# Four edits to a fused attention and MLP kernel: weight groups 3, 4, 3, 3, 3, relays on GpSimd, loads on SyncE, one early load on two queues

## The chip, the cores and the metric

The kernel runs on one core of a Trainium2 chip. The metric is the device time of one execution in microseconds; the median of three runs stands for the kernel. The trace is that of one profiled execution of the kernel before.

The engines are named as in the profile: PE is TensorE's matmul side and PEld its weight load, DVE is VectorE, ACT is ScalarE, POOL is GpSimd, SP is SyncE. SP, ACT and POOL also start DMA transfers, each from a queue that is worked through in order: an issue that has to wait holds up all that stand behind it on its engine.

## The reference

Talking-heads attention and, on its output, a two-matrix MLP with a parametrised ReLU. B = 4 batches, H = 12 heads, S = 448 positions, D = 64; the MLP has 1792 tokens, a model width of 768 and an inner width of 2048.

```python
scores = scale * np.matmul(q, k.transpose(0, 1, 3, 2))
scores = np.einsum('bhij,hg->bgij', scores, w_pre)        # mix over heads
scores = scores - np.max(scores, axis=-1, keepdims=True)
attn = np.exp(scores)
attn = attn / (np.sum(attn, axis=-1, keepdims=True) + 1e-09)
attn = np.einsum('bhij,hg->bgij', attn, w_post)           # mix over heads
x = np.matmul(attn, v)                                    # [B, H, S, D] -> [B*S, H*D]
h = x @ w_in
g = np.maximum(h, 0.0) + alpha * np.minimum(h, 0.0)
out = g @ w_out
```

The MLP's weights and alpha are given as float64.

## The kernel before, in words

**Attention.** A batch is cut into four chunks of query positions (120, 120, 120 and 90), 16 chunks in all. For a chunk, six score matmul pairs (Q, `qk`, L317) fill a tile `st` by way of PSUM copies (S, `qk_out`, L330). To mix over heads, the heads must lie on partitions: a relay (L, `relay`, L337) is an SBUF to SBUF DMA that brings ten positions of 12 heads, 120 rows of 448 floats (210 KB), from `st` into one of eight buffers `sr`. Two relays feed one mix (M, L344). There are 180 relays and 90 mixes. Behind a mix come the row maximum on DVE (R, L349), the exponential on ACT (E, L356), the normalised second mixing matrix on DVE (N, L362 to L366), the second mix with transposition on PE (P, `post`, L378), and copies into the tile `at` (A, L390). With all groups of a chunk done, V (`pv`, L400) multiplies by v; its result is split into a high and a low part (L414, L416) and stored in DRAM (`store_x`, L421).

The order of all of this is written out ahead by `plan`, a list scheduler with costs in us and priorities. It treats DMA as one engine; `emit` then issues each operation on a real queue. A relay goes to SP or POOL in turn (`relay_q`, L660). Loads of k (`load_k`, L279), q (`load_q`, L292) and v (`load_v`, L302) and the first three weights (`fetch`, L444) go to POOL; stores of x and of converted weights, and the loads of x and of converted weights for the MLP (L518, L548), go to SP. The planner gives a load a time, but on the chip a load waits only for its buffer and for what stands ahead of it in its queue. k has four buffers, q three, v three halves, the raw weights two.

Ahead of the plan the first chunk's q and all k of batch 0 are loaded by halves on SP and ACT (`hw`, L459 to L463). The second chunk's q follows on SP alone (L488).

**MLP.** The inner width is 16 blocks f of 128. A unit u is one f for one batch bl: `l1` (L577, 18 matmuls) computes h, four operations on ACT and DVE (L590 to L596) make g, `l2` (L615, 18 matmuls) adds to six PSUM accumulators. The f are grouped (`FGROUPS`, L39): a group runs all its f for one batch, adds the accumulators into SBUF (`l2_out`, L627), and goes to the next batch. There are 64 units in either grouping. On PE the order is l1(u), l2(u - 1), l1(u + 1) and so on. Unit u first needs f as the groups list it.

A weight is rounded from float64 to float32 and split into a high and a low part on DVE and ACT. The first NPRE = 3 blocks are made during the attention. The other 13 are made during the MLP by `convert2`: for each of w_in and w_out seven DVE operations (L59 to L65) and one split (L539 on ACT, L541 on DVE), so 16 steps to a block. There is room for five blocks. Block f with f % 5 = 0 takes the place of f - 5; the blocks with f % 5 = 1 and 2, and those with 3 and 4, share a tile and take the places of f - 5 and f - 4 together (`w_free`, L532). A tile is taken between the rounding and the split of w_in, when the last unit of the old blocks has been issued.

The steps are put between the units by credit. What a unit needs and is not yet done is issued ahead of it:

```python
def conv_ops(us):
    credit = min(credit + us, 4.0)
    while credit > 0 and conv_at < NFC:
        r = next(conv2)              # None: the tile is not free yet
        ...
        credit -= 0.95
...
    while conv_at <= units[u][2] and units[u][2] >= NPRE:
        conv_ops(0.95)               # ahead of l1(u)
...
            conv_ops(0.95)           # within the unit
        conv_ops(2.6)                # behind it
```

Raw weights of `convert2` are fetched by POOL (`fetch_w`, L427), two passes ahead. The x of a batch is loaded from DRAM into one of three tiles (`load_x`, L511) when the first unit of a batch before it starts.

Of the kernel before, what the change touches and what calls it, by code (L numbers as in the profile page):

```python
# [20 lines left out]
DM, DFF = 768, 2048  # L21
# [14 lines left out]
RAHEAD = 3  # L36
LAG = 2
WARM = (12, 8)
FGROUPS = [[0, 1, 2], [3, 4, 5], [6, 7, 8], [9, 10, 11], [12, 13, 14, 15]]  # L39
NPRE = 3  # L40
NWP = 4
NXS = 3
# [179 lines left out]
def talking_heads_prelu(ctx: ExitStack, tc: tile.TileContext, q, k, v, w_pre, w_post, mask, w_in, w_out, alpha, out):  # L222
    nc = tc.nc
# [48 lines left out]
    def load_k(b, kk, hfs=(-1, 0, 1), parts=((0, 2),), dmas=None):  # L272
        if -1 in hfs:
            k_t[b, kk] = kp.tile([128, 2, S], F32, tag="k", name=f"k{b}_{kk}")
        t = k_t[b, kk]
        for p0, p1_ in parts:
            for hf in [i for i in hfs if i >= 0]:
                dma = dmas[hf] if dmas else nc.gpsimd
                dma.dma_start(out=t[64 * hf:64 * hf + 64, p0:p1_, :],  # L279
                              in_=k[b, :, (NP * hf + 2 * kk + p0) * S:(NP * hf + 2 * kk + p1_) * S])  # L280

    def load_q(ci, hfs=(-1, 0, 1), dmas=None):
        b, c = chunk_list[ci]
        c0, cn = CHUNKS[c]
        if -1 in hfs:
            q_t[ci] = qp.tile([128, NP * CW], F32, tag="q", name=f"q{ci}")
            pad = 64 + MIN_M - cn
            if pad > 0:
                nc.gpsimd.memset(q_t[ci][:, NP * cn:NP * cn + pad], 0.0)
        for hf in [i for i in hfs if i >= 0]:  # L290
            dma = dmas[hf] if dmas else nc.gpsimd
            dma.dma_start(out=q_t[ci][64 * hf:64 * hf + 64, :NP * cn],  # L292
                          in_=q[b, :, QOFF[c] + NP * hf * cn:QOFF[c] + NP * (hf + 1) * cn])

    def load_v(b, hx, s):
        if s < 0:
            v_t[b, hx] = vp.tile([128, NS, DM // 2], F32, tag="v", name=f"v{b}_{hx}")
            return
        n = min(S - 128 * s, 128)
        if n < 128:  # L300
            nc.gpsimd.memset(v_t[b, hx][n:, s, :], 0.0)
        nc.gpsimd.dma_start(out=v_t[b, hx][:n, s, :], in_=v[b, 128 * s:128 * s + n, hx * DM // 2:(hx + 1) * DM // 2])  # L302

    u_t = {}

# [28 lines left out]
    def relay(n, dma, sr):  # L334
        ci, r = groups[n]
        sr_t[n] = sr_b[sr]
        dma.dma_start(out=sr_t[n][SR0:SR0 + GP], in_=s_t[ci][r:CHUNKS[chunk_list[ci][1]][1]:CHUNKS[chunk_list[ci][1]][1] // GI])  # L337
# [98 lines left out]
    conv = {}  # L436

    def fetch(i, k):
        f, x = half(i)
        if k < 0:  # L440
            conv[i] = [cvp.tile([128, DM], I64, tag="cr", name=f"cr{f}_{x}")]
            return
        n = slice(k * DM // NWP, (k + 1) * DM // NWP)
        nc.gpsimd.dma_start(out=conv[i][0][:, n], in_=(w_in, w_out)[x][f][:, n])  # L444

    def conv_op(i, j):
        if j == 0:
# [9 lines left out]
    with tc.manual_schedule():  # L457
# [3 lines left out]
        load_k(0, 0, parts=((0, 1), (1, 2)), dmas=hw)  # L461
        load_k(0, 1, dmas=hw)
        load_k(0, 2, dmas=hw)  # L463

        warm = start.tile([128, S], F32R, tag="warm", bufs=1, name="warm")
        nc.vector.memset(warm.bitcast(F32), 0.0)
# [16 lines left out]
        for i, w in enumerate((w_pre, w_post)):  # L483
            for p in ((SR0, 64), (0, 64))[i]:
                nc.gpsimd.dma_start(out=mask_sb[p:p + HP, i], in_=mask[:HP, :HI, :])
                nc.gpsimd.dma_start(out=wb[p:p + HP, i, :],
                                    in_=w.rearrange("(o h) g -> o h g", o=1).to_broadcast([HI, H, H]))
        load_q(1, dmas=(nc.sync, nc.sync))  # L488
        nc.gpsimd.dma_start(out=alpha_sb, in_=alpha)
        P2 = {}  # L490
        p2 = ctx.enter_context(ExitStack())
# [153 lines left out]
        turns = [0]  # L645
# [11 lines left out]
            )  # L657

        def relay_q(n, sr):
            relay(n, (nc.sync, nc.gpsimd)[turns[0] % 2], sr)  # L660
            turns[0] += 1
            if turns[0] == 1:
                matrices()
            if turns[0] == 2 * RAHEAD:
                nc.vector.tensor_scalar(out=oma, in0=alpha_sb, scalar1=-1.0, scalar2=1.0, op0=ALU.mult, op1=ALU.add)
# [118 lines left out]
```

## Time and profile before

| what | us |
|---|---|
| median of 3 runs | 864.59 (863.59 to 872.91) |
| profiled execution | 864.0 |
| its span | 861.5 |
| PE busy | 810.8 |
| DVE busy | 576.6 |
| ACT busy | 341.8 |
| POOL busy | 134.5 |

The span is the time between the first and the last instruction in the trace; 2.5 us of the execution lie around it. A window row gives for a stretch of the span the busy time of each engine with its number of instructions, the clock that TensorE was granted (1.00 is 2.4 GHz, 0.50 is 1.2 GHz), the mean busy share of the 16 DMA engines and what they moved. A wait row names the engine and line that waited, what released it, and the total, the number and the longest. A timeline row gives start, duration, instruction and, in brackets, the idle time before it with its releaser. The chain follows the last instruction back to what released it, step by step.

### The profile page before, as it was taken

Reading aid. Unit: us, or ns where it says so; the run is one execution under the profiler, and the core shown is the slowest. Engines: PE = TensorE matmul, PEld = TensorE weight load, DVE = VectorE, ACT = ScalarE, POOL = GpSimd, SP = SyncE. Lnnn points to the kernel's source line nnn. Section 1 sums busy time; section 2 is a strip of 40 time slices with the busy share of each in tenths; the row PEclk is TensorE's granted clock in tenths of the full one; section 3 lists DMA queues with packets and bytes.
Section 4 is the critical chain, followed back from the end, with each engine's and each line's share of the span. In section 5 each row is a group of like instructions: output and inputs, shape, how many; then the busy total and the mean of one; then the engine's idle time right before and its main releaser. Section 6 shows DMA issues by size and latency. Waiting matters only on the chain.

```text
span 861.5 us, 23937 instructions
## 1 busy us (share of the span) xinstructions
PE 810.8 (94%) x10380; PEld 654.2 (76%) x10380; DVE 576.6 (67%) x1029; ACT 341.8 (40%) x712; POOL 134.5 (16%) x243
## 2 busy tenths in 40 slices
PE   7679999989899999899999999999999999799998
PEld 3336666666566667689999999999999998689997
DVE  4678888877678878766555666676667646961332
ACT  3456767757666775542222211212121212111111
POOL 3443334323333221000000000000000000000000
PEclk9799999999999999999999999999999999989999
DMA  6899778969786778978211511251125111240111
GB/s 144 205 206 255 217 221 219 243 195 246 206 218 191 215 212 248 261 202 294 74 37 37 202 38 37 74 202 37 38 74 170 69 37 37 74 159 33 65 65 64
DMA packets 75036, 125.36 MB, mean 146 GB/s; under 512 B 33876, under 2 KB 63588, under 8 KB 74932
## 3 DMA queue, kind: packets, MB, share of 16 engines
q1 hardware_dynamic: 57636, 63.91, 24.5%
q0 software_dynamic: 16896, 59.07, 24.1%
q8 instruction: 81, 1.33, 0.7%
q10 hardware_dynamic: 400, 0.87, 0.4%
q14 instruction: 23, 0.19, 0.1%
HBM read 66.16 MB, written 18.92 MB: 99 GB/s over the span
## 4 chain that ended last, share of the span: by engine, by line
PE 77%; DVE 8%; DMA 7%; ACT 5%; issue 2%; SPq 0%; POOL 0%; DVEq 0%; ACTq 0%
PE h L577 27%; PE acc L615 26%; PE x L400 8%; PE pa L378 7%; DMA sr<-st 5%; PE m L344 5%; PE s L317 4%; DVE at L390 2%; ACT at L390 2%; ACT e L356 2%; DVE nm L349 2%; ACT st L330 1%; DMA k<-in_k_dram 1%; DVE ao L627 1%; DMA q<-in_q_dram 0%
## 5 line engine op out<-in xcount | busy, mean ns | idle before, releaser
L577 PE MATMUL h<-x,w 128*128 128x448 f32 x1152 | 250.5, 370 | 6.5 <-ACT w L539 6.4
L615 PE MATMUL acc<-g,w 128*128 128x448 f32 x1152 | 245.5, 366 | 0.6 <-DVE g L596 0.6
L577 PEld LDWEIGHTS h<-x,w 128*128 128x128 f32 x1152 | 217.3, 189 | 28.8 <-ACT w L539 6.8
L615 PEld LDWEIGHTS acc<-g,w 128*128 128x128 f32 x1152 | 216.1, 188 | 20.0 <-DVE g L596 1.0
L378 PEld LDWEIGHTS pa<-r,e 64*64 64x64 f32 x5040 | 98.5, 135 | 68.4 <-DVE at L390 27.5
L592 DVE SCALAR_TENSOR_TENSOR t<-t,oma,h 128x448 f32<-128x448 f32 x64 | 43.5, 680 | 153.8 <-ACT t L590 153.8
L590 ACT ACTIVATE t<-h 128x448 f32<-128x448 f32 x64 | 34.9, 545 | 263.6 <-PE h L577 263.6
L356 ACT ACTIVATE e<-m,nm 128x448 f32<-128x448 f32 x180 | 112.7, 634 | 40.2 <-DVE nm L349 26.5
L378 PE MATMUL pa<-r,e 64*64 64x60 f32 x5040 | 105.4, 223 | 18.3 <-issue 6.7
L349 DVE TENSOR_REDUCE nm<-m 128x2 f32<-128x896 f32 x90 | 97.1, 1083 | 12.0 <-PE m L344 11.8
L344 PE MATMUL m<-sr,wk 64*64 64x448 f32 x720 | 92.1, 563 | 11.6 <-DMA sr<-st 10.0
L317 PE MATMUL s<-k,q 64*64 64x448 f32 (+2 forms) x768 | 97.5, 564 | 5.5 <-ACT e L356 2.4
L400 PEld LDWEIGHTS x<-at,v 128*64 128x64 f32 x1536 | 74.5, 137 | 20.1 <-ACT e L356 11.2
L337 POOL DMA_DIRECT2D sr<-st x90 | 55.5, 618 | 201.6 <-PE m L344 135.5
L400 PE MATMUL x<-at,v 128*64 128x120 f32 (+1 forms) x1536 | 81.4, 263 | 2.9 <-ACT e L356 2.9
L390 DVE COPY at<-pa 128x480 f32<-128x480 f32 x89 | 57.7, 655 | 34.8 <-ACT at L390 31.3
L330 ACT COPY st<-s 120x896 f32<-120x896 f32 (+1 forms) x68 | 61.5, 908 | 26.7 <-PE s L317 25.6
L390 ACT COPY at<-pa 128x480 f32<-128x480 f32 x91 | 51.2, 570 | 51.3 <-PE pa L378 38.5
L594 ACT CAST g<-t 128x448 fp32r<-128x448 f32 x64 | 36.3, 567 | 53.3 <-DVE t L592 53.3
L627 DVE TENSOR_TENSOR ao<-ao,acc 128x448 f32<-128x448 f32 x96 | 52.7, 615 | 1.7 <-PE acc L615 1.7
L317 PEld LDWEIGHTS s<-k,q 64*64 64x64 f32 (+2 forms) x768 | 29.4, 130 | 30.4 <-issue 12.2
L344 PEld LDWEIGHTS m<-sr,wk 64*64 64x64 f32 (+1 forms) x720 | 24.8, 135 | 33.4 <-ACT e L356 9.3
(51 smaller groups left out, 539.7 us busy)
## 6 DMA issues: line engine op xcount, KB each, us to landing
sr<-st SPq DMA_DIRECT2D x90, 210.0 KB
sr<-st POOLq DMA_DIRECT2D x90, 210.0 KB, 5.5
x<-x SPq DMA_DIRECT2D x12, 1344.0 KB
cr<-in_w_in_dram POOLq DMA_DIRECT2D x13, 768.0 KB, 4.5
cr<-in_w_out_dram POOLq DMA_DIRECT2D x13, 768.0 KB, 4.6
x<-xe SPq DMA_DIRECT2D x48, 180.0 KB
x<-x SPq DMA_DIRECT2D x24, 224.0 KB
out_dram<-ao SPq DMA_DIRECT2D x24, 224.0 KB
```

Of the source, the lines that this page charges most:

```text
L317: nc.tensor.matmul(ps[i0:i1, hf, :S], q_t[ci][r, p * cn + i0:p * cn + i1], k_t[b, p // 2][r, p % 2, :], start=True, stop=True)
L330: copy(dst[:cn, p], u_t.pop(("qk", ci, p))[:cn, :, :S])
L337: dma.dma_start(out=sr_t[n][SR0:SR0 + GP], in_=s_t[ci][r:CHUNKS[chunk_list[ci][1]][1]:CHUNKS[chunk_list[ci][1]][1] // GI])
L344: nc.tensor.matmul(ps[hf:hf + 64, u, :S], wk[r, :], g[r, :], start=True, stop=True)
L349: nc.vector.tensor_reduce(out=nm, in_=m_t[m][:, :, :S], axis=AX.X, op=ALU.max, negate=True)
L356: nc.scalar.activation(out=e_t[m][:, u], in_=m_t[m][:, u, :S], func=AF.Exp, bias=nm_t[m][:, u:u + 1], scale=1.0, accum_out=se_t[m][:, u:u ...
L378: nc.tensor.matmul(dst[:, :, HI * u:HI * u + HI], e[h, u, 64 * jb:64 * jb + 64], r[h, u].rearrange("p (h i) -> p h i", h=H), start=True, s ...
L390: copy_on[eng](dst, pa[:, g, :NS * GP].rearrange("p (s i) -> p s i", i=GI))
L400: nc.tensor.matmul(ps[64 * t:64 * t + 64, 0, cl * CW:cl * CW + cn], v_t[b, hx][:, s, (2 * cl + t) * D:(2 * cl + t + 1) * D], a_t[ci][:, s, ...
L577: nc.tensor.matmul(ps[:, :S], w[:, tw, cc * 128:(cc + 1) * 128], x[:, tx, cc, :], start=(i == 0), stop=(i == 3 * NCC - 1))
L615: nc.tensor.matmul(accs[c][:, :S], w[:, tw, c * 128:(c + 1) * 128], g[:, tg], start=(f == fs[0] and i == 0), stop=(f == fs[-1] and i == 2))
L627: nc.vector.tensor_tensor(acc_sb[c, bl], acc_sb[c, bl], accs[c][:, :S], ALU.add)
```

## The change

- The groups of f become 3, 4, 3, 3, 3 blocks instead of 3, 3, 3, 3, 4.
- All relays are issued by POOL; before, SP and POOL took turns.
- All loads of k, q and v in the plan and the loads of the first three weights are issued by SP; before, by POOL. `fetch_w`, for the other 13 weights, stays on POOL.
- The second chunk's q is issued right behind the k loads, one half on SP and one on ACT; before, both halves on SP.

```diff
--- before.py
+++ after.py
@@ -36,7 +36,7 @@
 RAHEAD = 3
 LAG = 2
 WARM = (12, 8)
-FGROUPS = [[0, 1, 2], [3, 4, 5], [6, 7, 8], [9, 10, 11], [12, 13, 14, 15]]
+FGROUPS = [[0, 1, 2], [3, 4, 5, 6], [7, 8, 9], [10, 11, 12], [13, 14, 15]]
 NPRE = 3
 NWP = 4
 NXS = 3
@@ -275,7 +275,7 @@
         t = k_t[b, kk]
         for p0, p1_ in parts:
             for hf in [i for i in hfs if i >= 0]:
-                dma = dmas[hf] if dmas else nc.gpsimd
+                dma = dmas[hf] if dmas else nc.sync
                 dma.dma_start(out=t[64 * hf:64 * hf + 64, p0:p1_, :],
                               in_=k[b, :, (NP * hf + 2 * kk + p0) * S:(NP * hf + 2 * kk + p1_) * S])
 
@@ -288,7 +288,7 @@
             if pad > 0:
                 nc.gpsimd.memset(q_t[ci][:, NP * cn:NP * cn + pad], 0.0)
         for hf in [i for i in hfs if i >= 0]:
-            dma = dmas[hf] if dmas else nc.gpsimd
+            dma = dmas[hf] if dmas else nc.sync
             dma.dma_start(out=q_t[ci][64 * hf:64 * hf + 64, :NP * cn],
                           in_=q[b, :, QOFF[c] + NP * hf * cn:QOFF[c] + NP * (hf + 1) * cn])
 
@@ -299,7 +299,7 @@
         n = min(S - 128 * s, 128)
         if n < 128:
             nc.gpsimd.memset(v_t[b, hx][n:, s, :], 0.0)
-        nc.gpsimd.dma_start(out=v_t[b, hx][:n, s, :], in_=v[b, 128 * s:128 * s + n, hx * DM // 2:(hx + 1) * DM // 2])
+        nc.sync.dma_start(out=v_t[b, hx][:n, s, :], in_=v[b, 128 * s:128 * s + n, hx * DM // 2:(hx + 1) * DM // 2])
 
     u_t = {}
 
@@ -441,7 +441,7 @@
             conv[i] = [cvp.tile([128, DM], I64, tag="cr", name=f"cr{f}_{x}")]
             return
         n = slice(k * DM // NWP, (k + 1) * DM // NWP)
-        nc.gpsimd.dma_start(out=conv[i][0][:, n], in_=(w_in, w_out)[x][f][:, n])
+        nc.sync.dma_start(out=conv[i][0][:, n], in_=(w_in, w_out)[x][f][:, n])
 
     def conv_op(i, j):
         if j == 0:
@@ -461,6 +461,7 @@
         load_k(0, 0, parts=((0, 1), (1, 2)), dmas=hw)
         load_k(0, 1, dmas=hw)
         load_k(0, 2, dmas=hw)
+        load_q(1, dmas=hw)
 
         warm = start.tile([128, S], F32R, tag="warm", bufs=1, name="warm")
         nc.vector.memset(warm.bitcast(F32), 0.0)
@@ -485,7 +486,6 @@
                 nc.gpsimd.dma_start(out=mask_sb[p:p + HP, i], in_=mask[:HP, :HI, :])
                 nc.gpsimd.dma_start(out=wb[p:p + HP, i, :],
                                     in_=w.rearrange("(o h) g -> o h g", o=1).to_broadcast([HI, H, H]))
-        load_q(1, dmas=(nc.sync, nc.sync))
         nc.gpsimd.dma_start(out=alpha_sb, in_=alpha)
         P2 = {}
         p2 = ctx.enter_context(ExitStack())
@@ -657,7 +657,7 @@
             )
 
         def relay_q(n, sr):
-            relay(n, (nc.sync, nc.gpsimd)[turns[0] % 2], sr)
+            relay(n, nc.gpsimd, sr)
             turns[0] += 1
             if turns[0] == 1:
                 matrices()
```

## Rows read from the trace of the kernel before

**Rows 1.** Busy us by stage: window, PE PEld DVE ACT POOL, PEclk, DMA share, GB/s

```profile
16.00:33.00 17.00, 9.22 (x118) 3.96 (x114) 7.88 (x15) 5.19 (x12) 5.77 (x11) 0.70 0.78 193
33.00:70.00 37.00, 30.57 (x716) 17.66 (x712) 30.10 (x62) 21.61 (x55) 19.10 (x34) 0.95 0.87 209
70.00:371.00 301.00, 279.43 (x7081) 188.94 (x7078) 242.50 (x487) 206.94 (x469) 90.34 (x159) 0.99 0.80 223
```

**Rows 2.** Waits of PE, 16 to 70 us, then 20 to 371: total, times, longest

```profile
PE m L344 <- DMA sr<-st: 9.5, 4, 3.0
...
PE m L344 <- DMA sr<-st: 10.0, 5, 3.0
```

**Rows 3.** Chain that ended last, 10 to 70 us: start, us, what

```profile
4.64 7.46 DMA k<-in_k_dram
...
18.16 11.39 DMA sr<-st
...
49.74 14.79 DMA sr<-st
```

**Rows 4.** Timeline of PE at three mixes: start, us, instructions, idle before

```profile
29.59 1.77 PE L344 MATMUL m<-sr,wk 64*64 64x448 f32 x8 [3.01 <-DMA sr<-st]
...
32.63 0.62 PE L344 MATMUL m<-sr,wk 64*64 64x448 f32 x2
...
64.67 0.98 PE L344 MATMUL m<-sr,wk 64*64 64x448 f32 x8 [1.74 <-DMA sr<-st]
```

**Rows 5.** DMA issues from 16 to 70 us: queue, count, KB, us to landing

```profile
sr<-st POOLq DMA_DIRECT2D x16, 210.0 KB, 7.9
```

**Rows 6.** The chain in the MLP: L577 of units 2, 14 and 63

```profile
386.32 3.65 PE h L577 x18
...
474.89 3.71 PE h L577 x18
...
846.58 3.71 PE h L577 x18
```

**Rows 7.** Timeline of PE at units 47, 48, 50 and 51

```profile
718.53 3.88 PE L577 MATMUL h<-x,w 128*128 128x448 f32 x18
...
726.82 3.81 PE L577 MATMUL h<-x,w 128*128 128x448 f32 x18
...
742.17 3.14 PEld L577 LDWEIGHTS h<-x,w 128*128 128x128 f32 x16 [0.43 <-DVE w L541]
...
755.74 5.90 PE L577 MATMUL h<-x,w 128*128 128x448 f32 x18 [6.40 <-ACT w L539]
```

**Rows 8.** Busy by window, columns as before, at unit 51

```profile
755.00:758.00 3.00, 2.26 (x5) 1.66 (x6) 2.28 (x4) 0.69 (x1) 0.00 (x0) 0.50 0.00 0
```

**Rows 9.** Instructions of tile sr: duration ns min/median/max, first and last start

```profile
L337 SPq DMA_DIRECT2D sr<-st x90: 768/799/3007, 16.3 to 350.0; - x90
L337 POOL DMA_DIRECT2D sr<-st x90: 573/622/798, 16.6 to 352.7; - x90
```

**Rows 10.** Timelines of SP, POOL and ACT at the start

```profile
5.15 1.82 SPq L292 DMA_DIRECT2D q<-in_q_dram  x2
...
16.55 2.35 POOL L337 DMA_DIRECT2D sr<-st  x4 [9.48 <-ACT st L330]
...
7.77 0.91 ACT L330 COPY st<-s 120x896 f32<-120x896 f32 x1 [2.04 <-PE s L317]
```

**Rows 11.** Busy by window, columns as before, before the first relays

```profile
12.00:16.00 4.00, 3.68 (x36) 1.75 (x40) 1.09 (x1) 2.03 (x3) 0.00 (x0) 1.00 0.04 7
```

**Rows 12.** Timeline around unit 14, all engines

```profile
473.74 0.95 DVE L64 SCALAR_TENSOR_TENSOR ce<-cr,ce 128x768 int32<-128x768 int32 x1
...
475.72 0.84 ACT L539 CAST w<-ct 128x768 fp32r<-128x768 f32 x1 [2.55 <-DVE ct L65]
...
482.11 3.88 PE L577 MATMUL h<-x,w 128*128 128x448 f32 x18
482.47 0.56 DVE L63 TENSOR_SCALAR ce<-ce 128x768 int32<-128x768 int32 x1
```

## The prediction

> **What bounds the kernel now.** I read the stage windows first. TensorE (PE) is busy 279.43 of 301 us in the body of the attention and nearly all the time in the MLP. Two stretches are worse [rows 1]. From 16 to 33 us it is busy 9.22 of 17 us at a granted clock of 0.70. From 33 to 70 us it is busy 30.57 of 37 us at 0.95, and the DMA engines are then 0.87 busy. So the DMA change can pay in those 54 us; elsewhere it has to find something to shorten.
>
> The waits say what is missing there. In the whole attention the mix matmuls (L344) wait 10.0 us for relays, and 9.5 us of that lie before 70 us [rows 2]. The chain shows which relays: one issued at 18.16 took 11.39 us and released the third mix at 29.59; one issued at 49.74 took 14.79 us and released the mix at 64.67 [rows 3, 4]. Both follow an issue of SyncE (SP) in the chain. Of the relays on GpSimd (POOL) in the same stretch the median landing is 7.9 us [rows 5]. So the late relay of a pair is SP's. The trace gives no landing for SP's others.
>
> The MLP runs in units of two PE stretches (L577, L615), and the chain gives the pitch: 386.32 for unit 2 and 474.89 for unit 14, so 7.38 us [rows 6]. Unit 63 would start at 386.32 + 61 x 7.38 = 836.5; it starts at 846.58. So 10.1 us are lost, and the rows show where: around unit 47 (726.82 - 718.53 = 8.29, 0.9 over the pitch), at unit 50 (0.43), and at unit 51, where L577 waits 6.40 us for a converted weight and then takes 5.90 us instead of 3.9, at a granted clock of 0.50 [rows 7, 8].
>
> **The change part by part.**
>
> *Relays to GpSimd.* An issue costs 799 ns on SP and 622 on POOL [rows 9]. POOL gains 90 relays (56 us) and gives up 102 loads of nearly the same length, so POOL stays as idle as it is; no term. What moves is what each relay queues behind. Now SP and POOL each hold relays and other work in one order; afterwards a relay has only relays ahead of it on its queue, and only the sharing of the DMA engines delays it.
>
> *Loads to SP.* POOL's loads stand behind its first four relays, and these wait for ScalarE's scores until 16.55 [rows 10]. So the DMA engines stand idle from 12 to 16 us (share 0.04) [rows 11]. Afterwards SP, whose last load now goes out by 6.97 [rows 10], runs on, as far as its buffers are free: by the tile sizes in the code, q of chunks 2 and 3 (720 KB), v of batch 0 (1344), the first weight (768) and the fourth k tile (448), some 3.3 MB, until the second k load of batch 1 waits for chunk 3's score matmuls. At about 200 GB/s [rows 1], 0.9 MB of it go out in the idle 4 us. The other 2.4 MB run against the first eight relays (8 x 210 KB = 1.7 MB).
>
> Cost at the start: now the fourth mix, which takes the last two, starts at 32.63 [rows 4]. With half of 200 GB/s, 1.7 MB take 17 us from 16.5, to 33.5: no change. With two thirds, to 29.3; at best all the start's waits go, -7.8 (9.5 less the 1.74 at 64.67). With all loads first, 2.4 MB or +12 us, less what runs beside the eight relays already now: 193 GB/s over 17 us are 3.3 MB, less 1.7 and 0.4 for the next pair is 1.2 MB or 6 us. So +6. POOL's median of 7.9 against SP's 11.39 leans to POOL having a little over half. I take **-1.0**, ends -7.8 and +6.
>
> Gain after it: these loads are then gone from 33 to 56 us, and no relay stands in SP's queue. At the body's pace (279.43/301 = 0.93 busy) the 30.57 us of work need 32.9 us, not 37: -4.1. The lower clock costs 5% of 37, of which I give back a fifth, -0.4. So **-4.5**, ends 0 (the pipeline's own latency sets the pace) and -8.3 (no idle time, full clock). Nobody else is late there: VectorE's mix-to-exp chain follows the mixes.
>
> From 70 to 371 us: only 0.5 of the 10.0 us lie here, so there is nothing for an earlier relay to shorten. The k and v loads that wait for a free buffer now stand in SP's queue, and behind them stand stores and loads instead of relays. The stores' tiles are two deep, and v and k are asked for many us ahead. **0**, ends -3 and +3.
>
> *q of chunk 1 on two queues.* One issue of about 0.8 us is added to ScalarE ahead of its table load; ScalarE's first copy at 7.77 waits 2.04 us for PE [rows 10], which covers it. But its 180 KB now compete with SP's last k load, which lands at 12.10 and releases PE [rows 3]. At 200 GB/s that is up to +0.9; **+0.4**.
>
> *Groups 3, 4, 3, 3, 3.* Conversion of weights f = 3 to 15 is emitted at 3.55 us of credit per unit, 0.95 per step, 3.7 steps; a weight has 16 steps, so 4.3 units. What is missing when a unit asks for its weight is emitted at once, ahead of it. I counted these steps for both group lists from the code. Before: 7 at unit 50 and 12 at unit 51, because f = 13 and 14 take over the tile of f = 8 and 9, which is free only after unit 45. After: that burst is gone (2 steps at unit 54). But f = 6 is now due at unit 15, and 13 units give three weights: 12 steps at unit 15. And f = 8 now waits for the tile of f = 3 and 4 until unit 25, f = 11 for that of 6 and 7 until unit 37; each repeats the pattern of units 46 to 50, with 7 steps at units 30 and 42.
>
> Price of unit 15, from the same place of before [rows 12]: its L577 would start at 482.11. VectorE starts the last paced step at 482.47 and ends it at 483.03. Then two steps of 0.96 with their gaps, to 485.04, as between 473.74 and 475.72, and ScalarE's 0.84: 485.9. PE waits 3.8 us, then 0.43 for the low half as at unit 50. A clock drop as at unit 51 costs 5.90 - 3.88 - 0.43 = 1.6. Sum 5.8. Twice 0.9 and twice 0.43 for the repeated pattern: 2.7. Together 8.5 for the 10.1 now: **-1.5** rounded, ends -7.4 (VectorE's idle time swallows unit 15's burst) and +1.5 (unit 15 waits as long as unit 51 did).
>
> **Sum** against the profiled execution's 864.0 (span 861.5): -1.0 - 4.5 + 0 + 0.4 - 1.5 = -6.6, so **857.4**. The median of the runs shown is 864.59, 0.6 above it.
>
> *Two rules of the skill.* The rows show SP's relays landing late. The Trainium skill (DMA: Bandwidth & Descriptors, Why a DMA increments its semaphore by 16 and not by 1) says that a transfer is cut over the largest number of DMA engines up to 16 that divides the slowest dimension of both sides, that SP always takes the lowest-numbered ones and GpSimd rotates. By it a relay, 10 rows into 120 partitions, would run on 10 engines, from SP always the same 10, which makes the move a relief of these; the ramp would go to its -8.3 and the sum to 853.6. No row here shows single engines. Against the change speaks the skill's SBUF — State Buffer (SBUF: two separate sides): VectorE operations of a two-port mode lock GpSimd out of writing descriptors. The rows for POOL's relays, 573/622/798 ns beside all of VectorE's work [rows 9], allow it at most 0.18 us a relay; it has 0.02 of rival C's chance.
>
> **Rivals.**
>
> *A, the gain is larger (0.18).* Relays alone on a queue land in 5 us from the start; the ramp gives -8, the start -4, the burst at unit 15 half its price, -4. Time about **848 to 852**. For it: the chain's 11.39 and 14.79. Against: 2.4 MB of loads still run beside the first relays.
>
> *B, nothing moves (0.27).* The ramp from 33 to 70 us is the latency of mix, maximum, exp and post, not DMA, and the MLP's stall only moves from unit 51 to 15. For it: of the 9.5 us only 1.74 lie behind 33 us [rows 4]. Time **861 to 866**.
>
> *C, slower (0.12).* SP's loads, in flight since 6 us, hold the DMA engines while all relays share one queue. The fourth mix then starts up to 6 us later, with the granted clock low meanwhile as it is now. It decides from the point where relays get less than half of the 200 GB/s; at a third, with the ramp giving nothing back, 864.0 + 6 + 0.4 - 1.5 = **869**, and up to 875 if the clock stays low with it. For it: the 0.78 and 0.87 DMA shares leave little room. Against: the same loads run there already in part.
>
> The forecast itself has 0.43, its own range 853 to 861.
>
> **How the numbers follow.** A measurement of this kernel can tell about 1%, 8.6 us, from no change. Faster by more than that needs less than 856: all of A and four tenths of the forecast, 0.18 + 0.17 = 0.35. Slower needs over 873: half of C, and 0.05 for a wait that no row shows, 0.11. The rest is 0.54. For 8 in 10 the range takes the forecast, B and most of A and part of C: 849 to 868.
>
> **What would show it.** Right: the third and fourth mix start at 29 and 32 us, as now or a little earlier; the mix waits for relays fall below 6 us; the DMA share from 12 to 16 us is near 1 and from 40 to 56 below 0.8; PE in 33 to 70 us is over 33 busy; L577 waits near 4 us at unit 15 and none at unit 51. Wrong: the fourth mix after 35 us (C); the ramp at 6 us of idle time as now (B); no wait at unit 15, or the clock at 1.00 behind it (A). A new wait of PE on k, v or x loads would break the 0 for the body.

## The result and the profile after

The changed kernel takes 876.01 us (median of four executions, 873.39 to 879.08) against 864.09 for the kernel before: 1.0134 times as long, 95% interval 1.0089 to 1.0178. It is slower: the interval lies above 1, and the time lies outside the forecast's range of 849 to 868. The profiled execution took 874.98 us with a span of 873.2.

The stage windows of after come first (window, busy us of PE, PEld, DVE, ACT, POOL, then granted clock, DMA share, GB/s), beside [rows 1] and [rows 11].

```profile
12.00:16.00 4.00, 4.00 (x42) 1.72 (x37) 2.08 (x2) 2.05 (x3) 0.54 (x1) 1.00 0.09 19
16.00:33.00 17.00, 11.11 (x139) 4.08 (x134) 8.66 (x18) 5.60 (x14) 6.82 (x14) 0.90 1.04 264
33.00:70.00 37.00, 30.30 (x705) 17.78 (x700) 28.79 (x60) 21.04 (x51) 12.14 (x23) 0.95 0.85 199
70.00:371.00 301.00, 271.28 (x6768) 181.44 (x6761) 235.15 (x471) 199.66 (x453) 88.43 (x157) 0.98 0.79 220
```

The start became better (PE 11.11 of 17 us where it was 9.22, clock 0.90 where it was 0.70). The ramp is as it was. The body, where I had put a zero, does 6768 matmuls in the 301 us in which before did 7081. Nearly all of the time is lost there; in the ramp only the start's lead goes, as told below. The chain in the MLP says the same (start, us, what); unit 2, unit 15, the last stretch of unit 26, unit 28 and unit 63:

```profile
399.77 3.71 PE h L577 x18
...
500.44 5.04 PE h L577 x16
...
595.12 3.51 PE acc L615 x16
598.64 3.66 PE h L577 x18
...
858.53 3.71 PE h L577 x18
```

Against [rows 6], unit 2 starts 399.77 - 386.32 = 13.45 us later, and unit 63 only 858.53 - 846.58 = 11.95 later. So the MLP gained 1.50 us, as was forecast, and the attention lost 13.45.

What holds PE up in the attention is in the table of its waits, 0 to 385 us (what was waited for: us in total, times, longest). First after:

```profile
PE pa L378 <- issue: 14.1, 7, 3.9
...
PE m L344 <- DMA sr<-st: 5.3, 3, 4.2
...
PE x L400 <- issue: 2.0, 2, 1.1
...
PE m L344 <- issue: 1.5, 2, 0.9
...
PE s L317 <- issue: 1.0, 1, 1.0
```

The same table of before has one row with "issue":

```profile
PE pa L378 <- issue: 6.7, 7, 2.1
```

The waits for relays fell from 10.0 us [rows 2] to 5.3, as forecast. But "issue", time in which PE waits for nothing that the profile shows, rose from 6.7 to 14.1 + 2.0 + 1.5 + 1.0 = 18.6 us. One window each, from the start to unit 2 (before, then after), gives the account:

```profile
0.00:386.32 386.32, 346.57 (x8131) 231.08 (x8132) 297.70 (x592) 246.49 (x550) 121.82 (x219) 0.97 0.80 217
```

```profile
0.00:399.77 399.77, 354.59 (x8131) 234.64 (x8132) 298.20 (x592) 246.27 (x550) 114.53 (x207) 0.97 0.78 210
```

The matmuls are the same 8131. PE's idle time rose from 39.75 to 45.18 us: +11.9 of pauses, -4.7 of waits for relays, -1.8 of the rest. Its busy time rose by 8.02. Laying the two records matmul beside matmul shows where. Up to the 1000th matmul, at 74 us, the busy time rises by 3.7 us and the waits for relays fall by 4.2, so there the one about offsets the other. From the 1000th to unit 2 the changed kernel loses 13.1 us: the pauses rise by 10.2, the busy time by 4.4, of which 2.4 are the lower clock (1.2 GHz), and the other waits fall by 1.6. Between pauses both kernels keep step to the hundredth of a microsecond for stretches of 250 matmuls; 10.4 of the 13.1 us arise within 80 matmuls of a pause of one kernel or the other.

The longest pause shows how. The chain of after (start, us, what):

```profile
159.14 0.75 PE s L317 x8
159.89 0.76 PE pa L378 x39
160.66 3.86 issue
164.52 0.46 PE pa L378 x16
```

PE stops in the middle of a group of identical matmuls (39, then 16 more) whose operands are all there, so it is no wait for data. The windows around it:

```profile
157.00:160.00 3.00, 3.00 (x94) 1.86 (x93) 1.77 (x3) 0.60 (x2) 0.55 (x1) 1.00 1.08 267
160.00:163.00 3.00, 0.66 (x40) 0.52 (x30) 1.38 (x2) 0.88 (x1) 0.02 (x1) 1.00 1.03 269
163.00:166.00 3.00, 1.48 (x28) 0.75 (x32) 0.35 (x1) 0.96 (x2) 0.00 (x0) 0.97 0.77 233
166.00:170.00 4.00, 4.00 (x46) 3.06 (x40) 3.86 (x10) 2.89 (x8) 1.72 (x3) 0.59 0.49 159
```

The DMA engines are full (1.08, 1.03) when it happens, and behind the pause the granted clock is 0.59, so the next matmuls cost more too; not every pause is followed by a lower clock. The DMA queues name the missing thing. Of the stretch 155 to 162 us (queue, kind: packets, MB, share of 16 engines):

```profile
q0 software_dynamic: 369, 1.01, 58.9%
q1 hardware_dynamic: 476, 0.68, 45.4%
```

and of 161.5 to 164:

```profile
q1 hardware_dynamic: 714, 0.40, 56.5%
q0 software_dynamic: 148, 0.34, 44.9%
q8 instruction: 1, 0.02, 2.7%
```

q8 carries PE's instructions, a packet of 16 KB at a time. For seven microseconds up to 162 none comes; then one does (its packet runs from 162.11 to 163.19), and PE goes on at 164.52. The other pauses look alike. Of all 147 in the 17 kernels of the table below, each ends 1.2 to 1.8 us after such a page has landed, and they stand at the same places of PE's program in every kernel, to a few matmuls, some 126 matmuls apart or a multiple of that. Once started, a page's transfer takes 1.1 us at the median in before and after alike; so the delay lies ahead of the transfer. That the page waits behind relays and loads is inferred at this point, and tested below.

### The profile page after: what moved, and what is told of

Its sections match the earlier page's. It is cut to its first block, busy times and chain, and to the rows that moved or that the text cites. A ratio compares the mean times of both kernels' runs of the same rounds, so it can differ in the third digit from the quotient of the medians.

```text
span 873.2 us, 23928 instructions
## 1 busy us (share of the span) xinstructions
PE 819.1 (94%) x10380; PEld 657.5 (75%) x10380; DVE 577.9 (66%) x1029; ACT 341.6 (39%) x712; POOL 127.2 (15%) x231
## 3 DMA queue, kind: packets, MB, share of 16 engines
q0 software_dynamic: 18432, 59.30, 22.9%
q8 instruction: 82, 1.34, 0.7%
## 4 chain that ended last, share of the span: by engine, by line
PE 77%; DVE 9%; ACT 6%; issue 4%; DMA 3%; POOL 1%; SPq 0%; ACTq 0%; DVEq 0%; POOLq 0%
PE h L577 26%; PE acc L615 24%; PE x L400 9%; PE pa L378 8%; PE m L344 6%; PE s L317 5%; DVE at L390 2%; ACT at L390 2%; DMA sr<-st 2%; ACT e L356 2%; DVE nm L349 2%; DVE ao L627 1%; ACT st L330 1%; DMA k<-in_k_dram 1%; DVE ct L62 1%
## 5 line engine op out<-in xcount | busy, mean ns | idle before, releaser
L577 PE MATMUL h<-x,w 128*128 128x448 f32 x1152 | 250.5, 370 | 4.1 <-ACT w L539 3.7
L577 PEld LDWEIGHTS h<-x,w 128*128 128x128 f32 x1152 | 217.1, 189 | 26.7 <-ACT w L539 4.0
L378 PEld LDWEIGHTS pa<-r,e 64*64 64x64 f32 x5040 | 99.8, 137 | 74.6 <-issue 29.6
L337 POOL DMA_DIRECT2D sr<-st x180 | 103.9, 582 | 238.6 <-PE m L344 202.7
L378 PE MATMUL pa<-r,e 64*64 64x60 f32 x5040 | 107.6, 225 | 24.7 <-issue 14.1
L344 PE MATMUL m<-sr,wk 64*64 64x448 f32 x720 | 99.7, 571 | 9.0 <-DMA sr<-st 5.3
L344 PEld LDWEIGHTS m<-sr,wk 64*64 64x64 f32 (+1 forms) x720 | 26.5, 136 | 36.5 <-issue 18.7
L596 DVE TENSOR_TENSOR g<-t,g 128x448 fp32r<-128x448 f32 x64 | 39.9, 624 | 16.1 <-ACT g L594 16.1
```

The lines of the kernel that those rows point to most:

```text
L344: nc.tensor.matmul(ps[hf:hf + 64, u, :S], wk[r, :], g[r, :], start=True, stop=True)
L378: nc.tensor.matmul(dst[:, :, HI * u:HI * u + HI], e[h, u, 64 * jb:64 * jb + 64], r[h, u].rearrange("p (h i) -> p h i", h=H), start=True, s ...
L577: nc.tensor.matmul(ps[:, :S], w[:, tw, cc * 128:(cc + 1) * 128], x[:, tx, cc, :], start=(i == 0), stop=(i == 3 * NCC - 1))
```

## The experiments

All ratios are to the kernel before; for e1 to e15 it was measured on the same chip. "Pauses" are the rows "<- issue" of PE's waits to 385 us, "relay waits" the row "m <- DMA sr". For a third measure I took, for each of the first 58 pages, PE's place in its program when the page's transfer starts, and the earliest such place over all kernels. A page counts as late when its transfer starts over 2.5 us after PE passed that place; the limit is a choice, and another way to fix the place moves a count by up to four, but keeps the two groups named below apart. Pauses, relay waits and late pages are those of one profiled execution. For e2 and e14 that was the slowest of theirs, for e9 and e10 the fastest (876.59 us against a median of 870.40 in e2, 857.01 against 865.87 in e10), so the pauses of the first two stand high and those of the last two low. "Relays" is SyncE's and GpSimd's part in quarters.

| kernel | relays SP / POOL | loads | ratio [95%] | pauses | relay waits | late pages | unit 2 at |
|---|---|---|---|---|---|---|---|
| before | 2 / 2 | POOL | 1 | 6.7 | 10.0 | 7 | 386.3 |
| changed | 0 / 4 | SP | 1.0134 [1.0089, 1.0178] | 18.6 | 5.3 | 11 | 399.8 |
| e1_groups | 2 / 2 | POOL | 0.9985 [0.9944, 1.0025] | 9.4 | 8.9 | 6 | 386.2 |
| e8_q1 | 2 / 2 | POOL | 1.0018 [0.9983, 1.0053] | 8.1 | 7.4 | 5 | 385.6 |
| e3_loads | 2 / 2 | SP | 0.9928 [0.9892, 0.9964] | 4.6 | 5.9 | 5 | 380.9 |
| e2_relays | 0 / 4 | POOL | 1.0081 [1.0050, 1.0113] | 21.7 | 2.1 | 16 | 399.5 |
| e4_no_groups | 0 / 4 | SP | 1.0140 [1.0091, 1.0188] | 16.7 | 4.3 | 11 | 402.2 |
| e7_less_loads | 0 / 4 | SP, fewer | 0.9990 [0.9960, 1.0020] | 9.4 | 4.2 | 4 | 386.2 |
| e6_all_sp | 4 / 0 | POOL | 1.0177 [1.0110, 1.0245] | 7.4 | 12.5 | 6 | 398.8 |
| e5_wide | 2 wide / 2 | SP | 1.0003 [0.9974, 1.0031] | 9.3 | 0.2 | 10 | 383.1 |
| e15_wide_again | 2 wide / 2 | SP | 0.9994 [0.9954, 1.0033] | 15.3 | 0 | 10 | 386.1 |
| e13_wide_sp | 4 wide / 0 | POOL | 1.0070 [1.0027, 1.0113] | 15.9 | 3.6 | 10 | 394.2 |
| e10_undo_relays | 2 / 2 | SP | 0.9927 [0.9882, 0.9973] | 3.2 | 6.3 | 4 | 381.5 |
| e11_three_of_four | 1 / 3 | SP | 0.9972 [0.9930, 1.0013] | 8.1 | 3.4 | 2 | 385.8 |
| e12_act | 2 ACT / 2 | SP | 1.0071 [1.0029, 1.0114] | 3.3 | 7.2 | 2 | 393.1 |
| e14_pool_only | 0 / 4 | SP | 1.0201 [1.0136, 1.0267] | 21.1 | 4.5 | 12 | 408.8 |
| e9_six | 2 / 2 | SP | 0.9837 [0.9790, 0.9883] | 1.3 | 6.1 | 4 | 378.9 |

### The parts one by one

The kernel before with one part of the change each.

e1_groups:

```diff
-FGROUPS = [[0, 1, 2], [3, 4, 5], [6, 7, 8], [9, 10, 11], [12, 13, 14, 15]]
+FGROUPS = [[0, 1, 2], [3, 4, 5, 6], [7, 8, 9], [10, 11, 12], [13, 14, 15]]
```

> The kernel before with the new groups of f alone. The MLP of the changed kernel shows the forecast pattern (L577 waits 3.65 us at unit 15, small bursts at units 27 and 39), so theory A (the loss is TensorE pauses without a recorded wait in the attention, 18.6 us after against 6.7 before, and has nothing to do with the groups) expects 1.5 us less than before, 862 to 863. Theory B (the groups cost something outside the MLP, by shifting the weights' tiles) expects 870 or more.

e2_relays:

```diff
-            relay(n, (nc.sync, nc.gpsimd)[turns[0] % 2], sr)
+            relay(n, nc.gpsimd, sr)
```

> The kernel before with all relays on GpSimd and nothing else; loads stay on GpSimd, so they and the relays stand in one queue. If relays on GpSimd make TensorE's pauses (theory A1), 872 to 878 with 15 us or more of pauses. If SyncE's loads running ahead make them (theory A2), the pauses stay near 7 us; the start is a little worse, since eight relays and the loads share one queue: 864 to 868.

e3_loads:

```diff
-            dma = dmas[hf] if dmas else nc.gpsimd
+            dma = dmas[hf] if dmas else nc.sync
...
-        nc.gpsimd.dma_start(out=v_t[b, hx][:n, s, :], ...
+        nc.sync.dma_start(out=v_t[b, hx][:n, s, :], ...
...
-        nc.gpsimd.dma_start(out=conv[i][0][:, n], ...
+        nc.sync.dma_start(out=conv[i][0][:, n], ...
```

> The kernel before with the loads of k, q, v and of the first three weights on SyncE; relays still take turns. Theory A2 (loads sent as soon as their buffers are free pile up on the DMA engines) expects 872 to 878 with over 15 us of pauses, though here half the relays stand in SyncE's queue and hold the loads back a little; theory A1 expects the pauses near 7 us and 862 to 866.

e8_q1:

```diff
         load_k(0, 2, dmas=hw)
+        load_q(1, dmas=hw)
...
-        load_q(1, dmas=(nc.sync, nc.sync))
```

> The kernel before with the second chunk's q behind the k loads on two queues and nothing else. The changed kernel's first relays went out at 15.46 instead of 16.55 us. Expected: a start about 1 us earlier, 862 to 865, pauses near 7 us.

Groups and q move the time by less than can be told from nothing. The loads alone make the kernel faster, 0.9928. The relays alone make it slower, 1.0081, with fewer waits for relays than any kernel here with narrow relays (2.1 us) and with 21.7 us of pauses. So one part of the change carries the loss, and it is the one that does best what it was meant to do. The times of e2 and e3, 870.4 and 858.2 us, lie below what theory A1 had for them (872 to 878, 862 to 866); the pauses, over 15 us in the one and below 7 in the other, decide for it against A2.

e4_no_groups, the changed kernel with the old groups:

```diff
-FGROUPS = [[0, 1, 2], [3, 4, 5, 6], [7, 8, 9], [10, 11, 12], [13, 14, 15]]
+FGROUPS = [[0, 1, 2], [3, 4, 5], [6, 7, 8], [9, 10, 11], [12, 13, 14, 15]]
```

> The changed kernel with the groups of before: all three DMA edits. Theory A expects the changed kernel plus 1.5 us, 877 to 878, and the same pauses (18 to 19 us before 385 us). If the pauses fall where they do by chance of what happens to be in flight (theory C), they come out elsewhere and their sum differs by 5 us or more from 18.6, though nothing before the MLP is changed.

1.0140 against the changed kernel's 1.0134: the groups have no part in the loss that shows. Its pauses, 16.7 us, are a little fewer than the 18 to 19 expected, and most of them stand at the same places. Later I undid the relay part in the changed kernel, and moved the relays alone beside e3's loads.

e10_undo_relays (on the changed kernel) and e14_pool_only (on e3_loads, the edit the other way round):

```diff
-            relay(n, nc.gpsimd, sr)
+            relay(n, (nc.sync, nc.gpsimd)[turns[0] % 2], sr)
```

> The changed kernel with only its relay edit undone: relays alternate between SyncE and GpSimd again, loads on SyncE, groups 3, 4, 3, 3, 3, second chunk's q on two queues. Theory T1 (the relay edit carries the whole loss, through TensorE's pauses for the next page of its instructions): 855 to 860, pauses put down to issue before 385 us at 4 to 10 us against 18.6 of the changed kernel. Rival R (the loss is an interaction of the loads with groups or with q): 866 or more.

> The kernel before with all loads on SyncE and all relays on GpSimd, old groups, second chunk's q as before. Against the run with the loads alone it differs in 90 relays' queue only. Theory T1 (that move is the whole loss): ratio to before 1.010 to 1.017, pauses put down to issue 14 to 22 us before 385 us. Rival I (the loss needs q on two queues, or was a matter of that chip): ratio below 1.004.

Without the relay edit the changed kernel is at 0.9927, the same as e3. With it, e3 goes from 0.9928 to 1.0201; its waits read

```profile
PE pa L378 <- issue: 14.2, 8, 4.4
...
PE x L400 <- issue: 4.2, 4, 1.9
PE m L344 <- issue: 1.5, 1, 1.5
PE s L317 <- issue: 1.2, 2, 0.8
```

against this one in e10:

```profile
PE pa L378 <- issue: 3.2, 4, 1.3
```

So the relay move carries the whole loss, through the pauses and the clock behind them: of the 23.0 us that e14 loses against e3 from the 1000th matmul to unit 2, 15.4 are pauses and 6.5 the lower clock. That theory had 1.010 to 1.017 for e14; the measured 1.0201 is above it, though its interval reaches into it. How much the move costs depends on where the loads are: 0.8% with the loads on GpSimd (e2 against before), 2.7% with the loads on SyncE (e14 against e3). With the loads on GpSimd it gains at the start, where the fourth mix begins at 26.16 us instead of 32.63; with the loads on SyncE it does not (30.93 in e14, 30.09 in e3).

### Is it the load on the DMA engines?

e7_less_loads, the changed kernel without the k and v loads of batches 1 to 3 (the tiles of batch 0 are used again, so 8.3 MB less are moved by q1, and all batches are computed from the keys and values of the first):

```diff
+        if b > 0:
+            k_t[b, kk] = k_t[0, kk]
+            return
...
+        if b > 0:
+            v_t[b, hx] = v_t[0, hx]
+            return
```

> The changed kernel without the loads of k and v for batches 1 to 3; the tiles of batch 0 are used for all, so the result is not the reference's. About 9 MB of the 75 MB of the attention are gone, relays are untouched. If the pauses come from DMA engines that are busy when a program page is asked for, they fall well below 18.6 us, to 12 or less, and the time to 865 to 870. If they come from the relays' place alone, whatever else is in flight, they stay above 15 us.

0.9990 with 9.4 us of pauses: half of the pauses go with the 8.3 MB, and 0.014 of the ratio, some 12 us. PE's program is the same and its pages are as many. The pauses fell as the first theory had it (12 us or less), the time further (861.1 us for its 865 to 870). So a page is late because of what else the DMA engines have to move.

### Why the relay's queue matters

SyncE's and GpSimd's relays have the same bytes, but they are cut differently. The page's DMA queues show it; q1 of before, then of e2_relays, which takes 90 relays from it:

```profile
q1 hardware_dynamic: 57636, 63.91, 24.5%
```

```profile
q1 hardware_dynamic: 45936, 44.55, 16.3%
```

That is 11,700 packets, 130 for a relay: 120 rows and ten more, which would be one for each DMA engine that takes part. The Trainium skill (DMA: Bandwidth & Descriptors, Why a DMA increments its semaphore by 16 and not by 1) has such a relay on 10 engines, and the 130 agree with it. GpSimd's relays have 80 packets each (q0 has 18,432 in the changed kernel and 11,232 in e3), among them 40 of 5376 bytes and 16 completions in the packet records. So one theory was: while a SyncE relay is on the way, six engines are free for a page; GpSimd's take all.

The 16 completions don't show that GpSimd's relays take all engines: 40 equal packets can't be shared out evenly over 16 engines, and ten engines with four each, other engines from relay to relay, would fit as well. Where a relay's packets stand apart from others, at most 13 data packets of one GpSimd relay overlap in time, 14 of a narrow SyncE relay and 19 of a widened one of the kernels below. So one GpSimd relay looks no wider than SyncE's; whether successive ones go over different engines, no record shows.

What can be tested is the width of SyncE's relays. I let SyncE's relays of the 120-row chunks read another pattern: 120 rows of one head. The bytes are the same, the relayed scores are the wrong ones, and the cut is over 15 engines.

e5_wide and e15_wide_again (both on e3_loads), and e13_wide_sp (all relays on SyncE, on the kernel before):

```diff
     def relay(n, dma, sr):
         ci, r = groups[n]
         sr_t[n] = sr_b[sr]
+        if dma is nc.sync and CHUNKS[chunk_list[ci][1]][1] == GP:
+            dma.dma_start(out=sr_t[n][SR0:SR0 + GP], in_=s_t[ci][:GP, r])
+            return
```

> The kernel with the loads on SyncE (e3_loads: 858 us, 4.6 us of TensorE pauses without a recorded wait), in which SyncE's relays of the 120-wide chunks read 120 rows of one head instead of ten rows of twelve heads: same bytes, same 1792 byte pieces, same queue, but the relayed data are not the ones that the mix needs. Removing 90 relays from SyncE took 11,700 packets from its queue, 120 rows and 10 completions each, so a SyncE relay runs on 10 DMA engines; the Trainium skill's rule on how a transfer is cut (DMA: Bandwidth & Descriptors, Why a DMA increments its semaphore by 16 and not by 1) would put the wide form on 15. Theory N (TensorE's program pages come over a DMA engine that SyncE's relays leave alone and GpSimd's do not) expects 72 x 5 = 360 more packets under 512 B, pauses of 10 us or more and 864 to 872 us. Theory P (GpSimd's large packets hold the pages up) expects no change: 4 to 6 us of pauses, 856 to 860 us.

e6_all_sp, the kernel before with all relays on SyncE, narrow:

```diff
-            relay(n, (nc.sync, nc.gpsimd)[turns[0] % 2], sr)
+            relay(n, nc.sync, sr)
```

> The kernel before with all relays on SyncE, loads still on GpSimd. Theory N expects fewer pauses than before, under 6 us, and 858 to 863 us unless the start suffers. Theory P expects about the same or fewer pauses (half the relays' bytes leave GpSimd). A third theory (two queues share better than one, whichever they are) expects pauses as in the kernel with all relays on GpSimd, over 12 us, and 868 to 874 us.

> The kernel before with all relays on SyncE, loads on GpSimd as they were, and SyncE's relays of the 120-partition chunks read 120 rows of one head (the wrong scores are relayed, the bytes are the same), so that each is cut over 15 engines instead of 10. With narrow relays all on SyncE the pauses were 7.4 us and the ratio 1.018, most of it lost at the start where relays landed late. Theory W (relays on many DMA engines crowd out the pages, and half of them on few engines spare them): pauses of 12 us or more before 385 us, as with all relays on GpSimd, while the waits for relays fall from 12.5 to under 6 us; ratio 1.005 to 1.015. Theory V (it is GpSimd's way of writing its packets, 3 rows each of 5376 B): pauses under 9 us, waits for relays under 6 us, ratio 0.993 to 1.002.

> The kernel with loads on SyncE, alternating relays and SyncE's relays cut over 15 engines, a second time, beside the two others on one chip: it had ratio 1.0003 and pauses of 9.3 us. Theory W: between the loads alone (0.993) and all relays on GpSimd (1.014), 0.998 to 1.006, pauses 8 to 14 us. Theory V: 0.990 to 0.998, pauses under 8 us.

None of the three theories had e6's 877 us: its pauses are about those of before, and it loses at the start, where the fourth mix begins at 39.75 us instead of 32.63. But it makes a pair with e13: both have all relays on SyncE's queue and all loads on GpSimd's, and differ only in what 144 relays read, and so in the cut. Waits of e6, narrow:

```profile
PE m L344 <- DMA sr<-st: 12.5, 8, 3.7
PE pa L378 <- issue: 7.4, 4, 2.5
```

Waits of e13, wide (three lines were added in the relay's function, so L381 is L378 and L347 is L344):

```profile
PE pa L381 <- issue: 11.8, 6, 4.0
PE m L347 <- DMA sr<-st: 3.6, 2, 2.3
PE m L347 <- issue: 3.0, 1, 3.0
PE s L317 <- issue: 1.1, 1, 1.1
```

and their q1 on the page, e6 then e13:

```profile
q1 hardware_dynamic: 69336, 83.27, 29.0%
```

```profile
q1 hardware_dynamic: 70056, 83.27, 31.5%
```

The same bytes, and 720 packets more: five for each of the 144 relays that were widened, so 15 engines for 10. The relay waits fall from 12.5 to 3.6 us, and the pauses rise from 7.4 to 15.9, without one relay on GpSimd. So GpSimd's kind of packet isn't needed for the pauses, and all relays in one queue don't suffice for them. A relay that by these counts is on more engines lands sooner and delays the pages more. (The wide pattern also reads 120 rows of `st` where the narrow one reads ten; the runs don't part this from the number of engines.) In total e13 is still the faster of the two, 1.0070 against 1.0177: its fourth mix begins at 24.94 us instead of 39.75. e5 had 9.3 us of pauses and fell between the expectations; e15, the same kernel, had 15.3, so one profile tells a pause sum to some 6 us at best. The late pages are steadier: 2 to 7 in the nine kernels that have narrow relays, at least a quarter of them, and all loads, 10 to 16 in the seven with all loads that have only GpSimd's or widened ones (in e5, e13 and e15 SyncE's relays of the 120-row chunks are wide).

What stays open: no record names the engine that carried a packet, so that the pages passed on engines that the narrow relays left alone is inferred from counts. What GpSimd's relays do to the pages is shown (e2, e10, e14), by which engines they do it is not. And width is not all of it. With half the relays wide on SyncE the ratio is 1.000 (e5, e15), with all on GpSimd 1.020 (e14), at 10 to 12 late pages in each; why the rest of that loss needs all relays on GpSimd isn't settled.

### Doses and another queue

On e3_loads, one relay in four on SyncE, or ScalarE in SyncE's place:

```diff
-            relay(n, (nc.sync, nc.gpsimd)[turns[0] % 2], sr)
+            relay(n, nc.sync if turns[0] % 4 == 0 else nc.gpsimd, sr)      (e11)
+            relay(n, (nc.scalar, nc.gpsimd)[turns[0] % 2], sr)             (e12)
```

> The kernel before with all loads on SyncE and three of four relays on GpSimd, one on SyncE. With half of the relays on GpSimd it was 858.2, with all of them (old groups, q on two queues) 877.4. Theory D (the loss grows with the number of relays on GpSimd): 864 to 871, pauses put down to issue at 9 to 14 us before 385 us. Rival K (one relay in four on SyncE is enough to leave DMA engines free for the pages): 856 to 861, pauses under 7 us. Rival Q (any pair of successive relays on one queue is enough to lose): 873 to 880.

> The kernel before with all loads on SyncE, relays alternating between ScalarE's and GpSimd's queue, none on SyncE. Theory S (what matters is that each relay has another queue than the one before it): 856 to 864, plus up to 3 us for 90 more issues on ScalarE, so 856 to 867, pauses at 4 to 9 us before 385 us. Theory Y (what matters is that half of the relays stand in SyncE's order behind loads and stores, which spaces them in time): 870 to 880, pauses over 12 us. A loss without pauses would be ScalarE itself, held up by its relay's wait for the scores.

e11 lies between, 0.9972 with 8.1 us of pauses: half the narrow relays of e3 keep most of what they saved, so the loss is no straight line in the number moved. Both of these ran on a chip where the kernel before takes 870.59 us, so the microseconds of their expectations have to be read as ratios: 864 us would be 1.000 there. e12 has few pauses (3.3) and still 1.0071. Its relays leave SyncE's queue, so it is not SyncE's order that spares the pages. Its loss begins on ScalarE itself, as its timeline shows (ACTq is its instruction queue):

```profile
18.10 0.91 ACT L330 COPY st<-s 120x896 f32<-120x896 f32 x1
18.12 11.29 ACTq L337 DMA_DIRECT2D sr<-st  x3
29.47 0.63 ACT L356 ACTIVATE e<-m,nm 128x448 f32<-128x448 f32 x1 [10.46 <-DMA v<-in_v_dram]
```

The row merges three issues with what lies between them. The issues themselves take 0.8 to 1.6 us each; the third stands waiting before it goes out, as the instructions of the relay's line show:

```profile
L337 ACTq EVENT_SEMAPHORE  x1: 6027/6027/6027, 22.6 to 22.6; - x1
```

It is the ninth relay for eight buffers, so it needs a mix to free one. The first exponential stands behind it in ScalarE's order: at 22.64 in e3, it comes at 29.47. Laid beside e3's matmuls, e12 is 4.8 us behind by the 500th, at 51 us, and 12 by the end of the attention; what costs the other 7 wasn't traced.

### A faster kernel

The loads on SyncE, the relays alternating as before, and six groups, so that no weight waits for a tile that is freed late: e9_six, on e3_loads.

```diff
-FGROUPS = [[0, 1, 2], [3, 4, 5], [6, 7, 8], [9, 10, 11], [12, 13, 14, 15]]
+FGROUPS = [[0, 1, 2], [3, 4, 5], [6, 7, 8], [9, 10, 11], [12, 13], [14, 15]]
```

> The kernel before with all loads on SyncE and the relays left alternating (as in the run with the loads alone, 858.2), and with groups 3, 3, 3, 3, 2, 2. By the count of steps from the code no unit then finds 7 or 12 steps of conversion still to do, only 1, 3 and 3 at units 14, 26 and 38. Theory G (the MLP's losses are the steps emitted at once): the MLP loses some 2 us instead of 10.1, unit 63 stands about 8 us nearer to unit 2, no L577 waits over 1 us, and the time is 849 to 853, ratio 0.982 to 0.987. Rival (a smaller group costs elsewhere, since each group's first and last unit flush the accumulation and more partial sums are read back): 856 to 862.

0.9837 [0.9790, 0.9883], faster than both kernels, and as expected. In its chain unit 63 starts at

```profile
830.29 3.71 PE h L577 x18
```

and unit 2 at 378.85: 451.44 us for 61 units where before needs 460.26, 8.8 less. No L577 waits in its MLP any more, and the flushes of a sixth group cost nothing that shows.

## Why the prediction was wrong

**The body, 70 to 371 us: the step that failed.** I set it to 0, -3 to +3, because only 0.5 us of relay waits lie there. It cost +13.1: at the 1000th matmul, at 74 us, the changed kernel is 0.3 us behind, at unit 2 13.45. The argument looked for what an earlier relay could shorten and for loads that could come late. What it left out is that PE's own program comes over the same DMA engines, and that relays moved to GpSimd delay its pages: the pauses rose by 10.2 us there. The row for it was in before's table of waits: 6.7 us of "issue", seven times, second only to the relays' 10.0. I never asked what that was. A range of -3 to +3 for the body had no mechanism behind its upper end; a bound from that row, all pauses doubled, would have been +7, and still too small.

**The width of a relay.** The prediction had the rule that SyncE's relays run on 10 engines, and took it as a reason for a larger gain, the ramp going to -8.3. The packet counts bear the rule out; its sign here was the other one. The narrow relay was slow, and that was its use: widened on SyncE, it brought more pauses (e6 and e13, e3 and e15).

**The start: -1.0.** Right in sign. The first relays issue at 15.46 instead of 16.55, and the fourth mix starts at 30.21 instead of 32.63 [rows 4], as this row of the timeline shows:

```profile
30.21 1.84 PE L344 MATMUL m<-sr,wk 64*64 64x448 f32 x8
```

By the 250th matmul, at 33 us, the kernel is 1.76 us ahead. But the step behind the term failed, so the sign was partly luck. SP was to run on through its loads and fill the idle 4 us; the DMA share from 12 to 16 us is 0.09, where near 1 was to show it. SP's next load of q waited until 14.25 us, 6.9 us of it for PE's score matmuls, and the loads of v stand behind it in SP's order:

```profile
5.04 10.32 SPq L292 DMA_DIRECT2D q<-in_q_dram  x3
15.40 1.06 SPq L302 DMA_DIRECT2D v<-in_v_dram  x2
```

So rival C's loads ahead of the relays never came about, and its later fourth mix didn't either. (The amount was a little high as well: q of chunks 2 and 3 is 630 KB, not 720, as the fourth chunk has 90 positions.)

**The ramp: -4.5.** The DMA engines did get freer, 0.62 busy from 40 to 56 us where below 0.8 was forecast (0.97 before), but the gain didn't come: PE is busy 30.30 of 37 us, where over 33 was to show it, and by the 1000th matmul the lead is gone. Two things are in it. The term was too large: e3, e9 and e10, which have the move of the loads without that of the relays, gain 3.0, 2.2 and 1.3 us by the same matmul, start included. And a pause took what there was:

```profile
44.22 1.91 issue
```

The waits for relays, which were to fall below 6 us, fell to 5.3, and GpSimd's land in 7.4 us at the median from 16 to 70 us (7.9 in [rows 5]) though they now carry it all. So a step can do what it was to do and be worth little.

**q of chunk 1: +0.4.** e8 has 0.9983 to 1.0053, and can't tell it from zero.

**The MLP: -1.5.** Right, and in its parts. Unit 15, in the timeline of PE (start, us, instructions, idle before):

```profile
499.45 0.68 PE L577 MATMUL h<-x,w 128*128 128x448 f32 x2 [3.65 <-ACT w L539]
500.44 5.04 PE L577 MATMUL h<-x,w 128*128 128x448 f32 x16 [0.31 <-DVE w L541]
```

3.65 us for the 3.8 worked out, 0.31 for the 0.43, and 5.04 us for 16 matmuls where 18 take 3.71 at full clock, at a granted clock of 0.56 from 500 to 503 us. From unit 14 (488.41 in the chain) to unit 16 (509.12) it is 20.71 us, 5.9 over two pitches, where 5.8 was forecast. Unit 28 stands 15.62 behind unit 26, 0.86 over two pitches, where 0.9 was forecast for unit 27. Unit 51 has no wait. So steps counted from the code and priced from rows of the same pattern hold here to a tenth of a microsecond. The upper end of this term, +1.5, comes to +1.0 when its sum is redone; nothing hangs on it.

**The rivals.** None of the three was it. A and B assumed that relays earlier can't hurt. C had the right sign and nearly the size (869 to 875), by luck: at the wrong place and by another cause. The Trainium skill's rule on GpSimd's descriptors (SBUF — State Buffer, SBUF: two separate sides), weighed in C, shows nothing in the relays' issue times: they take 576 ns at the median, 806 at most.

## What to carry to other kernels

Read the "issue" rows of the busiest engine before moving DMAs: they may be its own program arriving late, and then the DMA engines are on its path even where every tensor is early. First see what has slack, and only then make it faster: a wider cut paid where the transfer was waited for (e13 against e6), and did not where there was slack (e5 and e15, at 1.000, against e3's 0.993). Where a term is set to 0 because nothing waits for the moved thing, ask what the thing will stand in front of.

## What the runs showed of the hardware

PE's program came in 82 pages of 16 KB (q8: 82 packets, 1.34 MB in the changed kernel). The Trainium skill (Runtime: NRT & Kernel Launch, Instruction fetch mechanics) gives the same 16 KB, has the sequencer fetch the next page over a DMA queue of its own while it executes the current one, and calls the cost mostly hidden. The pages agree; the cost doesn't. With the DMA engines 0.8 busy in the attention, pauses add up to 1.3 us in the best kernel here and 21.7 in the worst, single ones reach 4.4 us, and the granted clock can be low behind them (0.59 from 166 to 170 us). Where the same bytes are cut for 15 engines instead of 10, by the packet counts, the pauses rise from 7.4 to 15.9 us (e6, e13) and from 4.6 to 9.3 and 15.3 (e3, e5, e15).
